# A fused attention and MLP kernel: the MLP's inner rows turned by VectorE and sixteen small DMAs instead of by TensorE

## The chip, the cores and the metric

The kernel runs on one core of a Trainium2 chip. The metric is the device time of one execution in microseconds (us). The engines are named as the profile names them: PE is TensorE (PEld its weight loads), DVE is VectorE, ACT is ScalarE, POOL is GpSimd, and SP is the engine that issues nearly all of the DMAs. Each engine takes its instructions strictly in the order in which the program lists them.

## What is computed

Attention over 8 batches, 8 heads, 576 positions and 64 columns a head, with a mask in blocks of 64, and then an MLP over the 4608 tokens whose 512 columns are the eight heads side by side. Inputs of the MLP are `w_in` (512 x 1024), `w_out` (1024 x 512) and a gain `g_ln` of 1024.

```python
scores = scale * np.matmul(q, k.transpose(0, 1, 3, 2))
scores = np.where(pos[:, None] // 64 >= pos[None, :] // 64, scores, -1e9)
attn = softmax(scores)                       # exp(s - max) / (sum + 1e-9)
x = np.matmul(attn, v)                       # -> (4608 tokens, 512)
h = x @ w_in
solu = h * softmax(h)
ln = (solu - mean) / np.sqrt(var + 1e-6) * g_ln
out = ln @ w_out
```

Products of numbers in fp32 are made from two parts, a high one rounded to `fp32r` and a low one with the rest: high x high, high x low and low x high, so each product is three matmuls.

## The kernel before

**Units of work.** Attention is done for 32 pairs of heads (4 pairs to a batch), the MLP for 36 tiles of 128 tokens; 4.5 tiles are the tokens of a batch. Every piece of work is entered with `op(engine, estimated time, function, reads, writes, key)` into a `Schedule` (lines 67 to 195). It plays the program through with its estimates and, whenever an engine is free, gives it the ready piece with the lowest key; the keys are a table of numbers (`PARAMS`). Some pieces have alternatives on another engine (`alts`), and the planner gives the piece to whichever is free first. The order that comes out is the order of the program on each engine. PSUM is eight banks: two double ones ("D", for `h` and for the last block of scores) and four single ones ("S", for all the rest). A piece that opens a bank has to wait until all readers of the bank's last content are done.

**Attention** (`attention(p)`, lines 396 to 559). `q` and `k` are loaded by four DMAs each in runs of 32 floats (line 404) so that a transposition of 32x32 blocks by DVE (line 428) yields the whole transposed matrix. The high part is made by ACT (429) or POOL (430), the low part by DVE (432, 434). PE makes the scores (452 for the last block, 458 for the rest, in which the two heads use one half of the array's rows each); DVE sets the mask and takes the maximum (477, 481), ACT makes the exponentials (485), DVE the reciprocals of the sums (493, 494), POOL or DVE multiplies (501). PE transposes these in 25 blocks (512), ACT copies the result to SBUF (389), PE multiplies by `v` (545), and ACT copies that (389 again) into `xt[b % 3]`, the transposed input of the MLP, of which three batches are kept.

**The MLP** (`moe(t)`, lines 562 to 656). High and low part of the tile of `xt` go into `xh` and `xl` (577, 581; two buffers each). 24 matmuls make `h` in a double bank (602). DVE takes the maximum (608), ACT the exponential into `ub[t % 2]` (609), DVE multiplies by `h` and sums (610), POOL or DVE subtracts the mean (612, 613), and ACT squares and sums into a scrap tile `junk` (614). Then the row of 1024 has to be transposed for the second product: for each half of four 128x128 blocks PE transposes into a bank (637), ACT copies the high part into `ch` (641), and DVE makes the low part `cl` (642). `ch` and `cl` have one buffer. 24 matmuls make the output (650), ACT scales it into `ob[t % 2]` (654), and a DMA stores it (656).

**The weights** come as 64-bit floats. For each of 16 pieces a DMA (339) and about eight operations on ACT, DVE and POOL (341 to 359) make the parts `wih`, `wil`, `woh`, `wol`. This happens beside the attention of the first pairs, and its scratch lies in `xt[2]` and `ob`.

Of the kernel before, what the change touches and what calls it, by code (L numbers as in the profile page):

```python
# [31 lines left out]
NPT = 2  # L32
SWITCH = 165.0
# [10 lines left out]
    "a_xh": 88.845, "a_xl": 84.956, "a_c": -284.662, "a_o": -306.432, "np": 32, "l0": 61.467,  # L44
    "a_cl": -142.34, "a_ai": 313.132, "aff": -118.477, "a_t3": 111.852, "a_cm": -246.845, "a_cg": -26.262,
    "a_qh": -9.099, "a_kl": 129.132,
# [151 lines left out]
def kernel(  # L198
# [17 lines left out]
    P = 128  # L216
# [25 lines left out]
    qz, kz, qt, kt = (sb(x, [S]) for x in ("qz", "kz", "qt", "kt"))  # L242
    vr = [sb(f"vr{i}", [5, P]) for i in range(2)]


    qh, ql, kh, kl = ([sb(f"{x}{i}", [S], F32R) for i in range(2)] for x in ("qh", "ql", "kh", "kl"))
    qdh, qdl = ([sb(f"{x}{i}", [P], F32R) for i in range(2)] for x in ("qdh", "qdl"))
# [83 lines left out]
    xtf = xt[2].rearrange("p a b -> p (a b)")  # L331
    wtmp = [(xtf[:, 0:512], xtf[:, 512:1024], ob[0]), (xtf[:, 1024:1536], xtf[:, 1536:2048], ob[1])]
# [59 lines left out]
    def attention(p):  # L392
# [5 lines left out]
        half = [slice(0, 64), slice(64, 128)]  # L398
        for nm, src, dst in (("kz", k, kz), ("qz", q, qz)):

            def load(nm=nm, src=src, dst=dst):
                for g in range(4):
                    dma = ACT if p == 0 and nm == "kz" else SP
                    dma.dma_start(
                        dst[32 * g : 32 * g + 32, :].rearrange("p (g d) -> p g d", d=32),
                        src[b0, 2 * hp + g // 2, :, 32 * (g % 2) : 32 * (g % 2) + 32].rearrange("(g p) d -> p g d", p=32),
                    )

            op("SP", 1600, load, w=[nm], key=(K["l0"] if p == 0 else p) + K["ld" + sfx], tail=2400)
# [16 lines left out]
        qh_, ql_, kh_, kl_, qdh_, qdl_ = qh[i], ql[i], kh[i], kl[i], qdh[i], qdl[i]  # L426
        for x, z, t, hi, lo, scale in (("k", kz, kt, kh_, kl_, 1.0), ("q", qz, qt, qh_, ql_, 0.125)):
            op("DVE", t_dve(S), lambda z=z, t=t: DVE.transpose(t, z), r=[x + "z"], w=[x + "t"], key=kk)
            op("ACT", t_act(S), lambda t=t, hi=hi, scale=scale: ACT.activation(hi, t, AF.Copy, scale=scale), r=[x + "t"], w=[(x + "h", i)], key=ke,
               alts=[("POOL", 0.836 * S + 243, lambda t=t, hi=hi, scale=scale: POOL.tensor_scalar(out=hi, in0=t, scalar1=scale, scalar2=1.0, op0=ALU.mult, op1=ALU.mult), K["a_qh"])])  # L430
            if x == "q":
                op("DVE", t_dve(S), lambda: DVE.scalar_tensor_tensor(out=ql_, in0=qt, scalar=0.125, in1=qh_.bitcast(F32), op0=ALU.mult, op1=ALU.subtract), r=["qt", ("qh", i)], w=[("ql", i)], key=ke, port=True)  # L432
            else:
                op("DVE", t_dve(S), lambda: DVE.tensor_tensor(out=kl_, in0=kt, in1=kh_.bitcast(F32), op=ALU.subtract), r=["kt", ("kh", i)], w=[("kl", i)], key=ke, port=True,
# [6 lines left out]
        for x, dst, src in (("qh", qdh_, qh_), ("ql", qdl_, ql_)):  # L441
            op("POOL", 300, lambda dst=dst, src=src: last(dst, src), r=[(x, i)], w=[(x + "d", i)], key=ke)

        for g, (kind, us, masks) in enumerate(groups):
# [15 lines left out]
            if us == [LAST]:  # L460
                d, md = 3 * (t_mm(320) + t_mm(256)), 0
                rd = [(x, i) for x in ("kh", "kl", "qhd", "qld")]
                tiles = [(sps[0], [(LAST, 192)])]
            else:
                d, md = sum(3 * t_row(128 * (i_ + 1)) for i_, _ in us), 2
                rd = [(x, i) for x in ("kh", "kl", "qh", "ql")]
# [65 lines left out]
        x2 = wkeys if b0 == 2 else []  # L532
# [22 lines left out]
        for ph in range(2):  # L555
            av = avs[ph]
            for rows, parts in xparts[ph]:
                for c_, q_, l_ in parts:
                    copy(2, l_, lambda rows=rows, av=av, c_=c_, q_=q_, l_=l_: (xt[b0 % 3][rows, hp, q_ : q_ + l_], PS(av)[rows, c_ : c_ + l_]), 1.0, [("xt", b0 % 3, hp, rows.start, q_)], ke, av, x2)


    def moe(t, key):
# [3 lines left out]
        while a < (t + 1) * P:  # L566
            bb = a // S
            e = min((t + 1) * P, (bb + 1) * S)
            segs.append((bb % 3, a - bb * S, e - bb * S, a - t * P, e - t * P))
# [44 lines left out]
        op("ACT", t_act(1024, 135), lambda: ACT.activation(junk, u, AF.Square, accum_out=m[:, 4:5]), r=[uk], w=[("m4", i)], key=key + K["sq"])  # L614
# [15 lines left out]
        op("POOL", 702, rstd, r=[("m7", i), ("m5", i)], w=[("m4", i), ("m3", i)], key=key + K["sq"])  # L630
        for hf in range(2):
            cps = newps("S")

            def ctrans(hf=hf, cps=cps):
                t_ = PS(cps)
# [65 lines left out]
```

## Time and profile before

| | |
|---|---|
| median of 3 runs | 790.3 us (789.97 to 790.9) |
| the profiled execution | 790.35 us, of which the span of the profile is 788.6 us |
| mean granted PE clock | 0.975 of full |
| busy share of PE, PEld | 96%, 76% |
| busy share of DVE, ACT, POOL | 60%, 66%, 43% |
| DMA | 198551 packets, 47.05 MB |

The profile is of one execution. Its windows divide the span into stretches and give for each engine the busy time in it. Its groups give the mean duration of one instruction of a line. Its chain follows back from the last instruction to whatever released it; where PE never waits, the chain simply is PE's work, so that the spacing of equal points in it is the period of the work.

### The profile page before, as it was taken

To read this page: it belongs to the slowest core of one execution; us is meant where nothing else is said; L and a number is where in the kernel's file an instruction comes from. 1 tells how busy PE (TensorE), PEld (TensorE's weight loads), DVE (VectorE), ACT (ScalarE), POOL (GpSimd) and SP (SyncE) were. 2 spreads that over 40 slices of the span, in tenths; PEclk is the share of its full clock that TensorE was granted. 3 is DMA by queue.
4 is the path that set the end of the run, shared out by engine and by line. 5 is a ranking of instruction groups with operands and counts; after the bars stand their busy time and mean duration, and the time that the engine had idled before them with its cause. 6 is when DMAs were issued, how large, how long until landed. Compare 5 with 4: busy or idle time off the path is not lost.

```text
span 788.6 us, 13834 instructions
## 1 busy us (share of the span) xinstructions
PE 760.3 (96%) x4687; PEld 595.4 (76%) x4687; DVE 471.7 (60%) x1191; ACT 521.6 (66%) x1349; POOL 341.7 (43%) x593
## 2 busy tenths in 40 slices
PE   4878999999999999999999999999999999999998
PEld 3656776887777777777777777787777878888886
DVE  5889998955666555555555666655554534444442
ACT  5788989876677676666777667677666654443332
POOL 4766857645444444444444444444445131121100
PEclk8787999999999999999999999999999999999999
DMA  9764653322222222222222222222200100000001
GB/s 185 144 137 118 120 120 88 61 59 59 58 43 48 59 49 55 59 46 59 59 59 59 59 46 48 55 51 54 59 23 22 30 14 27 26 16 28 14 27 41
DMA packets 198551, 47.05 MB, mean 60 GB/s; under 512 B 191824, under 2 KB 191824, under 8 KB 198480
## 3 DMA queue, kind: packets, MB, share of 16 engines
q1 hardware_dynamic: 196112, 45.87, 26.9%
q8 instruction: 37, 0.61, 0.3%
q10 hardware_dynamic: 2368, 0.30, 0.3%
q14 instruction: 34, 0.28, 0.1%
HBM read 36.70 MB, written 9.44 MB: 59 GB/s over the span
## 4 chain that ended last, share of the span: by engine, by line
PE 86%; ACT 5%; DVE 4%; DMA 2%; issue 1%; POOL 1%; SPq 0%; DVEq 0%; ACTq 0%; POOLq 0%
PE ps L650 25%; PE ps L602 25%; PE ps L512 10%; PE ps L545 9%; PE ps L458 8%; PE ps L637 4%; PE ps L452 3%; ACT pb L485 2%; DVE nm L481 1%; DMA ub<-in_moe_w_out_dram 1%; DMA kz<-in_k_dram 1%; DMA ub<-in_moe_w_in_dram 1%; POOL pb L501 0%; ACT xt L389 0%; DVE ql L432 0%
## 5 line engine op out<-in xcount | busy, mean ns | idle before, releaser
L501 POOL TENSOR_SCALAR pb<-pb,rz 128x384 f32<-128x384 f32 (+4 forms) x288 | 176.6, 629 | 241.4 <-DVE rz L494 227.2
L485 ACT ACTIVATE pb<-ps,nm 128x256 f32<-128x256 f32 (+4 forms) x288 | 155.1, 548 | 47.3 <-DVE nm L481 46.6
L389 ACT ACTIVATE pt<-ps 128x512 f32<-128x512 f32 (+1 forms) x224 | 108.5, 562 | 42.0 <-PE ps L512 41.6
L642 DVE TENSOR_TENSOR cl<-ps,ch 128x512 fp32r<-128x512 f32 x72 | 49.4, 686 | 142.7 <-ACT ch L641 142.7
L481 DVE TENSOR_REDUCE nm<-ps 128x1 f32<-128x256 f32 (+4 forms) x288 | 131.4, 509 | 2.1 <-PE ps L452 2.1
L512 PE MATMUL ps<-ident,pb 128*128 128x128 f32 x800 | 111.2, 287 | 11.2 <-POOL pb L501 6.3
L512 PEld LDWEIGHTS ps<-ident,pb 128*128 128x128 f32 x800 | 93.9, 146 | 24.6 <-POOL pb L501 9.7
L545 PE MATMUL ps<-pt,vr 128*64 128x320 f32 (+4 forms) x896 | 93.8, 360 | 0.3 <-ACT pt L389 0.3
L545 PEld LDWEIGHTS ps<-pt,vr 128*64 128x64 f32 x896 | 59.3, 137 | 34.4 <-issue 1.3
L602 PE MATMUL ps<-wih,xh 128*128 128x512 f32 x288 | 84.7, 416 | 0.2 <-ACT pb L485 0.2
L650 PE MATMUL ps<-woh,ch 128*128 128x512 f32 x288 | 83.4, 411 | 0.0
L602 PE MATMUL ps<-wil,xh 128*128 128x512 f32 x288 | 79.8, 399 | 0.0
L650 PE MATMUL ps<-wol,ch 128*128 128x512 f32 x288 | 79.0, 396 | 0.0
L602 PE MATMUL ps<-wih,xl 128*128 128x512 f32 x288 | 78.8, 395 | 0.0
L650 PE MATMUL ps<-woh,cl 128*128 128x512 f32 x288 | 78.6, 394 | 0.0
L625 POOL TENSOR_TENSOR ms<-ms,mhalf 128x1 f32<-128x1 f32 x36 | 19.8, 549 | 131.8 <-DVE ms L622 131.7
L641 ACT ACTIVATE ch<-ps 128x512 fp32r<-128x512 f32 x72 | 44.0, 611 | 49.5 <-PE ps L637 49.5
L458 PE MATMUL ps<-kh,qh 64*128 64x256 f32 (+3 forms) x256 | 57.4, 395 | 10.5 <-POOL qh L430 5.4
L602 PEld LDWEIGHTS ps<-wil,xh 128*128 128x128 f32 x288 | 54.9, 190 | 13.0
L654 ACT ACTIVATE ob<-ps,ms 128x512 f32<-128x512 f32 x36 | 24.8, 688 | 60.0 <-PE ps L650 54.3
L602 PEld LDWEIGHTS ps<-wih,xl 128*128 128x128 f32 x288 | 54.4, 189 | 12.9
L650 PEld LDWEIGHTS ps<-wol,ch 128*128 128x128 f32 x288 | 54.3, 188 | 12.8
(83 smaller groups left out, 1275.5 us busy)
## 6 DMA issues: line engine op xcount, KB each, us to landing
qz<-in_q_dram SPq DMA_DIRECT2D x128, 72.0 KB, 2.5
out_dram<-ob SPq DMA_DIRECT2D x36, 256.0 KB, 2.0
kz<-in_k_dram SPq DMA_DIRECT2D x124, 72.0 KB, 2.5
vr<-in_v_dram SPq DMA_DIRECT2D x64, 128.0 KB, 2.6
ub<-in_moe_w_in_dram SPq DMA_DIRECT2D x8, 512.0 KB, 4.2
ub<-in_moe_w_out_dram SPq DMA_DIRECT2D x8, 512.0 KB, 3.7
vr<-in_v_dram SPq DMA_DIRECT2D x32, 32.0 KB, 2.4
kz<-in_k_dram ACTq DMA_DIRECT2D x4, 72.0 KB, 3.8
```

Of the source, the lines that this page charges most:

```text
L389: op("ACT", t_act(n_), lambda: ACT.activation(aps()[0], aps()[1], AF.Copy, scale=scale), r=r, w=w, key=key, ps=ps, alts=[("DVE", t_dve(n_) ...
L458: PE.matmul(PS(sps[h])[:, off : off + 128 * (i_ + 1)], w_[half[h], 128 * i_ : 128 * i_ + 128], x_[half[h], 0 : 128 * (i_ + 1)], start=n_ = ...
L481: op("DVE", t_dve(wid[u]), lambda sp=sp, off=off, u=u: DVE.tensor_reduce(out=nm_[u], in_=PS(sp)[:, off : off + wid[u]], axis=AX.X, op=ALU. ...
L485: op("ACT", t_act(wid[u], 186), lambda sp=sp, off=off, u=u, zg=zg, zc=zc: ACT.activation(pb[:, poff[u] : poff[u] + wid[u]], PS(sp)[:, off ...
L501: op("POOL", 0.836 * nn + 243, lambda b=b, nn=nn, zg=zg, zc=zc: POOL.tensor_scalar(out=pb[:, poff[b] : poff[b] + nn], in0=pb[:, poff[b] : ...
L512: PE.transpose(t[:, (s_ - c0) * P : (s_ - c0 + 1) * P], pb[:, poff[b] + j * P : poff[b] + (j + 1) * P], ident)
L545: PE.matmul(PS(avs[ph])[half[h], 64 * o_ : 64 * (o_ + n_)], vt[:, j, 64 * h : 64 * h + 64], pt_.rearrange("p s q -> p (s q)")[:, 128 * s_ ...
L602: PE.matmul(o_, a_[:, c, :], w_[:, c, s_], start=(si == 0 and c == 0), stop=(si == 2 and c == NKI - 1))
L637: PE.transpose(t_[:, c * P : (c + 1) * P], u[:, (4 * hf + c) * P : (4 * hf + c + 1) * P], ident)
L641: op("ACT", t_act(512), lambda cs=cs, cps=cps: ACT.activation(ch[:, cs, :].rearrange("p c q -> p (c q)"), PS(cps), AF.Copy), w=[("ch", hf) ...
L642: op("DVE", t_dve(512), lambda cs=cs, cps=cps: DVE.tensor_tensor(out=cl[:, cs, :].rearrange("p c q -> p (c q)"), in0=PS(cps), in1=ch[:, cs ...
L650: PE.matmul(o_, a_[:, c, :], w_[:, c, :], start=(hf == 0 and si == 0 and c == 0), stop=(hf == 1 and si == 2 and c == 7))
```

## The change

1. **Transposition in the MLP, tiles 6 to 33** (28 of 36). DVE transposes the row of 1024 in 32x32 blocks from `ub` into a new tile `zb` (one buffer). SP then issues 16 DMAs, each of 32 partitions x 256 floats (pieces of 1 KB), that carry the blocks to their partitions in a new tile `ct` (one buffer). ACT and DVE make `ch` and `cl` from `ct` in SBUF; POOL and DVE are alternatives for `ch`, POOL for `cl`. Tiles 0 to 5 and 34 and 35 keep PE's transpositions.
2. **Attention's results in two batches** instead of three: `xt[b % 2]`. So the results of batch b can be written only where the tiles of batch b-2 have been read.
3. **Scratch.** `junk` is dropped and the squares go into `ob[t % 2]`; the weights' scratch lies in `zb`, `ct` and `ob`.
4. **The first four pairs** load `q` and `k` in runs of 64 floats (two DMAs of 128x4x64, and one of 64x2x64 into `kq`) and PE transposes them (9 blocks a pair) instead of DVE; their high and low parts are then read from PSUM.
5. **The table of keys** is another one. With it the multiplications by the reciprocals (501) go mostly to DVE (none of 288 before, 205 now), the subtraction of the mean too (27 of 36 instead of 14), and 24 of the `kl` go to POOL.

The core of the diff:

```diff
+NQK = 2
+XB = 2
+PEQ = 4
+PET, PEL = 6, 34
 PARAMS = {
-    "nd": 2, "ld": -112.86, "lv": 9.571, "q": 88.586, "qe": 132.144, "s": 58.329, "se": -84.684,
+    "nd": 2, "ld": -336.409, "lv": -194.807, "q": 8.649, "qe": 317.465, "s": 21.981, "se": -51.803,
...
-    xt = [sb(f"xt{i}", [NP, S]) for i in range(3)]
+    xt = [sb(f"xt{i}", [NP, S]) for i in range(XB)]
...
+    zb = sb("zb", [DFF])
+    ct = sb("ct", [4, NKO, 32])
     ch = sb("ch", [NKO, P], F32R)
     cl = sb("cl", [NKO, P], F32R)
     ob = [sb(f"ob{i}", [DM]) for i in range(2)]
-    junk = sb("junk", [DFF], mybir.dt.bfloat16)
...
+                if peq:
+                    for h in range(2):
+                        dma.dma_start(
+                            dst[:, 0:512].rearrange("p (c d) -> p c d", c=4)[:, :, 64 * h : 64 * h + 64],
+                            src[b0, 2 * hp + h, 0:512, :].rearrange("(c p) d -> p c d", p=P),
+                        )
...
+            op("PE", 109 * 5, lambda: trans(kz, pk, True), r=["kz", "kzq", "qzq"], key=kk, opens=pk)
+            op("PE", 109 * 4, lambda: trans(qz, pq, False), r=["qz"], key=kk, opens=pq)
...
-        op("ACT", t_act(1024, 135), lambda: ACT.activation(junk, u, AF.Square, accum_out=m[:, 4:5]), r=[uk], w=[("m4", i)], key=key + K["sq"])
+        op("ACT", t_act(1024, 135), lambda: ACT.activation(ob[i].bitcast(mybir.dt.bfloat16), u, AF.Square, accum_out=m[:, 4:5]), r=[uk], w=[("m4", i), ("ob", i)], key=key + K["sq"])
...
+        if PET <= t < PEL:
+            op("DVE", t_dve(DFF), lambda: DVE.transpose(zb.rearrange("p (r c i) -> p r c i", r=4, i=32), u.rearrange("p (c r i) -> p r c i", r=4, i=32)), r=[uk] + (wkeys if t == PET else []), w=["zb"], key=key + K["ct"])
+
+            def place():
+                for r_ in range(4):
+                    for a_ in range(4):
+                        SP.dma_start(ct[32 * r_ : 32 * r_ + 32, a_, :, :], zb[32 * a_ : 32 * a_ + 32, 256 * r_ : 256 * r_ + 256])
+
+            op("SP", 2800, place, r=["zb"], w=["ct"], key=key + K["ct"], tail=2400)
         for hf in range(2):
+            cs = slice(hf * 4, hf * 4 + 4)
+            h_, l_ = (x[:, cs, :].rearrange("p c (a j) -> p a c j", a=4) for x in (ch, cl))
+            if PET <= t < PEL:
+                c_ = ct[:, :, cs, :]
+                op("ACT", t_act(512), lambda c_=c_, h_=h_: ACT.activation(h_, c_, AF.Copy), r=["ct"], w=[("ch", hf)], key=key + K["ce"],
...
+                op("DVE", t_dve(512), lambda c_=c_, h_=h_, l_=l_: DVE.tensor_tensor(out=l_, in0=c_, in1=h_.bitcast(F32), op=ALU.subtract), r=["ct", ("ch", hf)], w=[("cl", hf)], key=key + K["ce"], port=True,
...
+                continue
```

How it moves the instructions is shown at three places. The first is PE near the end of the program, when attention is over: the last matmuls of one tile's `h` (`xl_132`) and what stands between them and the next tile's `h` (`xh_129`). Before:

```order
L602 MATMUL ps_61<-wih,xl_132 128x512 x4
L650 MATMUL ps_65<-woh,ch 128x512 x4
L650 MATMUL ps_65<-wol,ch 128x512 x4
L650 MATMUL ps_65<-woh,cl 128x512 x4
L637 MATMUL ps_64<-ident,ub_133 128x128 x4
L650 MATMUL ps_65<-woh,ch 128x512 x4
L650 MATMUL ps_65<-wol,ch 128x512 x4
L650 MATMUL ps_65<-woh,cl 128x512 x4
L637 MATMUL ps_66<-ident,ub_133 128x128 x4
L602 MATMUL ps_62<-wih,xh_129 128x512 x4
```

And now:

```order
L640 MATMUL ps_61<-wih,xl_132 128x512 x4
L705 MATMUL ps_64<-woh,ch 128x512 x4
L705 MATMUL ps_64<-wol,ch 128x512 x4
L705 MATMUL ps_64<-woh,cl 128x512 x4
L705 MATMUL ps_64<-woh,ch 128x512 x4
L705 MATMUL ps_64<-wol,ch 128x512 x4
L705 MATMUL ps_64<-woh,cl 128x512 x4
L640 MATMUL ps_62<-wih,xh_129 128x512 x4
```

The two groups of four transpositions of `ub` are gone, so that PE's row is `h` of one tile and the output of an earlier one in turn. From the end of a tile's `h` to the start of its output there stand, as before, two outputs and two `h` of other tiles.

The second place is DVE in the same stretch. Before, from the multiplication of one tile (`ub_134`) to the maximum of the next (`ms_140`):

```order
L610 SCALAR_TENSOR_TENSOR ub_134,ms_141<-ps_61,ub_134 128x1024
L642 TENSOR_TENSOR cl<-ps_64,ch 128x512
L611 TENSOR_SCALAR ms_141<-ms_141 128x1
L613 TENSOR_SCALAR ub_134<-ub_134,ms_141 128x1024
L642 TENSOR_TENSOR cl<-ps_65,ch 128x512
L622 TENSOR_SCALAR ms_141<-ms_141 128x1
L608 TENSOR_REDUCE ms_140<-ps_62 128x1
```

And now:

```order
L648 SCALAR_TENSOR_TENSOR ub_134,ms_142<-ps_61,ub_134 128x1024
L686 TENSOR_TENSOR cl<-ct,ch 128x4x4x32
L649 TENSOR_SCALAR ms_142<-ms_142 128x1
L651 TENSOR_SCALAR ub_134<-ub_134,ms_142 128x1024
L686 TENSOR_TENSOR cl<-ct,ch 128x4x4x32
L670 STREAM_TRANSPOSE zb<-ub_134 128x1024
L660 TENSOR_SCALAR ms_142<-ms_142 128x1
L646 TENSOR_REDUCE ms_141<-ps_62 128x1
```

The two `cl` are of the tile before, whose blocks the DMAs have carried to `ct`; the transposition of this tile's row into `zb` comes behind them, since `zb` and `ct` have one buffer each.

The third place is SP's row in the middle of the program, where attention and MLP run beside each other. Before, one pair and one tile:

```order
L656 DMA out_dram<-ob_138 128x512
L404 DMA kz<-in_k_dram 32x18x32 x4
L404 DMA qz<-in_q_dram 32x18x32 x4
L413 DMA vr_83<-in_v_dram 128x4x64 x2
L417 DMA vr_83<-in_v_dram 64x2x64
L656 DMA out_dram<-ob_137 128x512
```

And now:

```order
L675 DMA ct<-zb 32x256 x16
L711 DMA out_dram<-ob_140 128x512
L434 DMA vr_83<-in_v_dram 128x4x64 x2
L438 DMA vr_83<-in_v_dram 64x2x64
L675 DMA ct<-zb 32x256 x16
L425 DMA kz<-in_k_dram 32x18x32 x4
L425 DMA qz<-in_q_dram 32x18x32 x4
L711 DMA out_dram<-ob_139 128x512
```

The sixteen DMAs stand ahead of the loads of a later pair, which cannot be issued before them.

More of the change, by code (lines that the diff above doesn't have):

```diff
@@ L428, in attention @@
+        for x, z, t, hi, lo, scale in () if peq else (("k", kz, kt, kh_, kl_, 1.0), ("q", qz, qt, qh_, ql_, 0.125)):
             op("DVE", t_dve(S), lambda z=z, t=t: DVE.transpose(t, z), r=[x + "z"], w=[x + "t"], key=kk)
-            op("ACT", t_act(S), lambda t=t, hi=hi, scale=scale: ACT.activation(hi, t, AF.Copy, scale=scale), r=[x + "t"], w=[(x + "h", i)], key=ke,
+            op("ACT", t_act(S), lambda t=t, hi=hi, scale=scale: ACT.activation(hi, t, AF.Copy, scale=scale), r=[x + "t"], w=[(x + "h", iq)], key=ke,
@@ L461, in attention @@
                 d, md = 3 * (t_mm(320) + t_mm(256)), 0
[L462 removed]
+                rd = [(x, iq) for x in ("kh", "kl", "qhd", "qld")]
                 tiles = [(sps[0], [(LAST, 192)])]
@@ L558, in attention @@
                 for c_, q_, l_ in parts:
-                    copy(2, l_, lambda rows=rows, av=av, c_=c_, q_=q_, l_=l_: (xt[b0 % 3][rows, hp, q_ : q_ + l_], PS(av)[rows, c_ : c_ + l_]), 1.0, [("xt", b0 % 3, hp, rows.start, q_)], ke, av, x2)
+                    copy(2, l_, lambda rows=rows, av=av, c_=c_, q_=q_, l_=l_: (xt[b0 % XB][rows, hp, q_ : q_ + l_], PS(av)[rows, c_ : c_ + l_]), 1.0, [("xt", b0 % XB, hp, rows.start, q_)], ke, av)
     def moe(t, key):
```

63 lines of the change are left out of this document (42 added, 21 removed), and 12 rows, old and new, of the table PARAMS.

## Prediction

> **What bounds the kernel now.** I read the page first (busy shares, then the chain of work that ended last), then the windows, to see where PE is not busy.
>
> ```profile
> PE 760.3 (96%) x4687; PEld 595.4 (76%) x4687; DVE 471.7 (60%) x1191; ACT 521.6 (66%) x1349; POOL 341.7 (43%) x593
> ...
> PE 86%; ACT 5%; DVE 4%; DMA 2%; issue 1%; POOL 1%; SPq 0%; DVEq 0%; ACTq 0%; POOLq 0%
> ```
>
> ```profile
> 0.00:160.00 160.00, 135.55 (x889) 102.93 (x890) 135.37 (x331) 130.22 (x357) 104.06 (x178) 0.88 0.59 122
> 160.00:620.00 460.00, 460.00 (x2982) 360.38 (x2981) 267.19 (x705) 321.44 (x859) 210.40 (x369) 1.00 0.25 51
> 620.00:784.00 164.00, 164.00 (x818) 131.83 (x817) 69.11 (x155) 69.28 (x135) 27.23 (x46) 1.00 0.06 23
> 664.10:676.16 12.06, 12.06 (x57) 9.84 (x57) 5.22 (x11) 4.76 (x9) 2.04 (x3) 1.00 0.06 22
> 341.14:362.58 21.44, 21.44 (x140) 16.80 (x140) 12.53 (x33) 14.99 (x42) 9.78 (x17) 1.00 0.27 54
> ```
>
> The columns of a window are its length and the busy time of PE, PEld, DVE, ACT and POOL, then granted clock, DMA share and GB/s. There are three stages. Up to 160 us PE is idle for 160.0 - 135.55 = 24.45 us at a mean clock of 0.88: the weights are being prepared and DVE (135.4) and ACT (130.2) are nearly full. From 160 to 784 PE is busy in all of it at full clock, first with a pair and a tile in 21.44 us (fifth row), then with tiles alone in 12.06 us (fourth row). In these 624 us only PE's own work counts: an instruction taken off PE is gain, unless something else then comes late.
>
> **What PE loses.** In the last stage the chain, in order of time, shows 24 matmuls of `h` as one piece, and the next one 12.06 us later.
>
> ```profile
> by line: PE ps L650 25.0%; PE ps L602 24.8%; PE ps L512 10.3%; PE ps L545 9.4%; PE ps L458 8.5%; PE ps L637 4.4%; PE ps L452 3.3%; ACT pb L485 2.3%; issue 1.4%; DVE nm L481 1.1%; DMA ub<-in_moe_w_out_dram 1.0%; DMA kz<-in_k_dram 0.7%; DMA u
> ...
> 664.10 5.58 PE ps L602 x24
> 676.16 5.59 PE ps L602 x24
> ```
>
> The output also has 24 matmuls of 512 columns, so it is worth 5.59 us too, and 12.06 - 2 x 5.59 = 0.88 us is left for the eight transpositions. The chain's shares give a second value: L637 with 4.4% of 788.6 is 34.7 us, 0.96 for each of 36 tiles. I take the lower one: 28 x 0.88 = 24.6 us less, all in the stages where PE is full. By the order, blocks of scores (the matmuls that use half the array's rows) begin 81 times now and 92 times before.
>
> ```profile
> PEld ps L458 <- issue: 24.0, 69, 0.4
> ```
>
> Weight loads stood idle for 24.0 / 69 = 0.35 us ahead of such a block. 11 fewer are 3.8 us if that is on PE's path and nothing if the matmul before hides it; I take 1.0.
>
> **What the others get.** A transposition of 576 takes 0.77 us and a maximum of 1024 takes 1.22.
>
> ```profile
> L428 DVE STREAM_TRANSPOSE qt<-qz 128x576 f32<-128x576 f32 x32 | 24.5, 766 | 1.1 <-DMA qz<-in_q_dram 0.8
> L608 DVE TENSOR_REDUCE ms<-ps 128x1 f32<-128x1024 f32 x36 | 43.8, 1216 | 31.1 <-PE ps L602 31.0
> L501 POOL TENSOR_SCALAR pb<-pb,rz 128x512 f32<-128x512 f32 x64 | 55.8, 884 | 9.2 <-DVE rz L494 4.2 <-ACT pt L389 1.7 <-PE ps L512 0.5
> L343 DVE TENSOR_SCALAR xt<-ub 128x512 f32<-128x512 f32 x9 | 3.8, 419 | 0.3 <-DMA ub<-in_moe_w_out_dram 0.3
> L642 DVE TENSOR_TENSOR cl<-ps,ch 128x512 fp32r<-128x512 f32 x72 | 49.4, 686 | 142.7 <-ACT ch L641 142.7
> L641 ACT ACTIVATE ch<-ps 128x512 fp32r<-128x512 f32 x72 | 44.0, 611 | 49.5 <-PE ps L637 49.5
> ```
>
> One of 1024 should take 1.24 us, 34.7 us in all. The 205 multiplications that come from POOL cost DVE at most about 0.42 us each (the 512 wide one; POOL needs 0.88), some 62 us over all widths. In the middle stage that is 1.24 + 2.0 us more a pair, less 0.6 for the `kl` that go: about 15.5 us of DVE in a period of 20.5 (12.53 of 21.44 before). It stays below PE's 20.5, so I cost it at nothing; that cover would be gone if DVE had to stand still for 5 us in every period. `ch` and `cl` read SBUF instead of PSUM; I leave them at 0.61 and 0.69.
>
> **The sixteen DMAs** are the unknown price. No DMA of before goes from SBUF to SBUF or has 32 rows. The nearest are these, with the time that SP spends on each issue (second column; the middle two rows hold four DMAs and one):
>
> ```profile
> 311.19 0.37 SPq L656 DMA_DIRECT2D out_dram<-ob  x1
> ...
> 319.57 1.93 SPq L404 DMA_DIRECT2D qz<-in_q_dram  x4
> ...
> 322.69 0.61 SPq L417 DMA_DIRECT2D vr<-in_v_dram  x1
> ```
>
> ```profile
> out_dram<-ob SPq DMA_DIRECT2D x36, 256.0 KB, 2.0
> ...
> vr<-in_v_dram SPq DMA_DIRECT2D x64, 128.0 KB, 2.6
> ```
>
> A plain store of 128 rows takes 0.37 us to issue and lands 2.0 us later; the worst, with three dimensions, takes 0.61, and 2.6 is a late landing. Sixteen in a row are then P = 16 x 0.37 + 2.0 = 7.9 us from `zb` to a whole `ct`, and 16 x 0.61 + 2.6 = 12.4 at worst. If an issue went with the number of rows it would be a quarter of 0.37, and P = 3.5. I take 7.9, since the store has the same plain form. The Trainium skill, on the page "DMA: Bandwidth & Descriptors", section "Issuing engines are not separate DMA queues", says that the sequencer's time to start a DMA is usually small beside the DMA itself. By that, P would be little over 2.0 and the two stall terms below would be zero; the rows above speak against it for sixteen issues in a row.
>
> Does P reach PE? In the last stage one tile's turn through `ct` is: P, `ch`, then the store's copy of the tile before, the second `ch`, `cl`, and the next transposition.
>
> ```profile
> 712.01 0.69 ACT L654 ACTIVATE ob<-ps,ms 128x512 f32<-128x512 f32 x1 [2.19 <-PE ps L650]
> ...
> 712.59 0.59 ACT L641 ACTIVATE ch<-ps 128x512 fp32r<-128x512 f32 x1
> 712.73 0.15 DVE L611 TENSOR_SCALAR ms<-ms 128x1 f32<-128x1 f32 x1 [1.91 <-ACT ob L654]
> 712.92 0.76 DVE L613 TENSOR_SCALAR ub<-ub,ms 128x1024 f32<-128x1024 f32 x1
> ```
>
> That is P + 0.61 + 0.69 + 0.59 + 0.69 + 1.24 and some 0.4 for handing over: P + 4.2 = 12.1 us, against 2 x 5.59 = 11.2 of PE. The turn is longer by 0.9 us, over the 8 tiles that are left then 7.4 us. The start has a reserve: between a tile's `h` and its output PE has four blocks, 4 x 5.59 = 22.4 us, and the way through maximum, exponential, product, mean, transposition, P, `ch`, `cl` sums up to about 17. So some 5.4 of the 7.4 are absorbed and 2.0 us remain.
>
> In the middle stage the turns come 15 to 20 us apart, so the turn itself does not bind; but DVE and ACT take their work in order, and while a `cl` waits for `ct`, the maxima of the scores queue behind it, and PE waits for those. By the order, in some nine of the 20 tiles there are only 4 to 8 us of DVE work between the transposition and its `cl`, where 7.9 + 0.6 are needed. The same wait is there before:
>
> ```profile
> DVE cl L642 <- ACT ch L641: 142.7, 27, 11.0
> ```
>
> DVE stood still 27 times at `cl`, up to 11.0 us, and PE was full all the while. So PE has work in hand for waits of this size; I take 2.0 us and keep 0 to 14.
>
> SP itself: the sixteen issues of 5.9 us stand ahead of loads of a pair (eight of 0.48 and three of `v`, about 6 us of issue). Together with 0.37 a store that is some 12 of 20 us. Loads may come 6 us later, but the buffers they fill are free a period ahead. The squares now also wait until the store of two tiles before has left `ob`, which it did a whole tile ago, and the weights' scratch in `zb` and `ct` is free before tile 6; both cost nothing.
>
> **The start.** PE makes 36 transpositions more in it; at 0.23 us (15 of them in 3.46) they are 8.3 us. DVE loses eight of 0.77, 6.2 us, and the first loads have half as many pieces.
>
> ```profile
> 1.70 3.46 PE L283 MATMUL ps<-ident 128*128 128x128 f32 x15 [1.70 <-POOL ident masks.py:199]
> ...
> PE ps L458 <- POOL qh L430: 5.4, 1, 5.4
> ```
>
> PE's first scores waited 5.4 us for `qh`, and PE has 24.45 idle us to hide in. Counting rows, DVE has the same work behind it at the same progress (ten pairs and four or five tiles) in both orders. I take 0, from -8 to +5.
>
> **Against the change** speaks the Trainium skill, page "VectorE: DVE Perf Modes", sections "The three transpose paths" and "Rules for kernel authors": VectorE's transposition stays within 32x32 blocks, and for a whole 128x128 one should use TensorE where PSUM will do as the target. Here the result was read from PSUM, so the page would keep it there; the trace has PE full for 624 us and DVE at 58%, and the page does not weigh that. By it alone nothing would be gained, about 790.
>
> **The sum**, against the profiled execution's 790.35 us (its span of 788.6 and 1.75 around it; the median of the runs is 790.3): 790.35 - 24.6 - 1.0 + 0 + 2.0 + 2.0 = 768.75, or 768.8.
>
> **Rivals.**
> - *The start gets shorter.* Shorter loads and multiplications of half the time shorten the chain of the first pairs by the 5 to 8 us above: 768.8 - 7 = 762. Against it stands that DVE and ACT are nearly full there anyway.
> - *Half the gain is given back in the middle stage,* to 781. With two batches, the last copies into `xt` of a batch's first two pairs have to wait for a tile two batches back, and hold two of four single banks of PSUM meanwhile; by the order that is about 30 us long at pair 24. With two banks left, a group of four transpositions of 0.44 us comes round every (0.44 + 0.6 + 0.4) / 2 = 0.72 us, 0.28 later each; 13 groups are 3.6 us a batch, about 12 where it happens in three or four of the six batches it can. For it speaks that DVE is at 76% and has less time to catch up.
> - *Slower: the issue costs what the worst row says.* P = 12.4 makes the turn 16.6 us, 5.4 over PE's 11.2: 8 x 5.4 - 5.4 = 38 us, and 1 us for each of 20 tiles before: 790.35 - 25.6 + 58 = 823. The gain is eaten from about 8 x (turn - 11.2) - 5.4 + 4 = 26 on, a turn of 14.6 and P = 10.4, which is 0.5 us an issue. Against it: plain forms took 0.37.
> - *The gain is eaten just so,* within 790 +- 1.6, by an issue of about 0.5 us; here the rule of the transpose paths would put it.
>
> **How the numbers follow.** Forecast 0.58 (763 to 776), shorter start 0.10, half given back 0.20 (774 to 787), slower 0.09, no change 0.03. Faster by more than 0.2% (1.6 us, about what a measurement of this kernel can tell) is 0.58 + 0.10 + 0.20 = 0.88. The range leaves out slower, no change, and the outer half of the shorter start: 757 to 786. The predicted time is the forecast's, 768.8.
>
> **What the profile after would show.** PE full from about 160 us to the end; the chain with L637's successor at 1% (8 tiles and the last copies) instead of 4.4%; two equal points of the last stage 11.2 to 11.5 us apart; about 20.5 us for a pair and a tile; sixteen issues in some 6 us on SP and a landing about 2 us later. I would be wrong if the last stage's period is over 12 us, if PE waits for maxima or for `pt` in the middle stage for more than 5 us in all, if the sixteen issues take over 8 us, or if PE's idle time before 160 us moves by more than 8 us.

## The result, and the profile after

| | before | after |
|---|---|---|
| median | 790.1 us (788.0 to 790.9, 4 runs) | 856.5 us (854.1 to 859.8, 4 runs) |
| profiled execution, span | 790.35, 788.6 us | 857.65, 855.8 us |
| mean granted PE clock | 0.975 | 0.938 |

The ratio is 1.085 with a 95% interval of 1.080 to 1.089: 66 us slower, where 21.5 less were forecast. The page of the kernel after, busy shares, the chain by engine and the issue of the new DMAs:

```profile
PE 776.1 (91%) x4499; PEld 598.1 (70%) x4499; DVE 565.1 (66%) x1404; ACT 525.9 (61%) x1355; POOL 236.7 (28%) x402
...
PE 36%; SPq 21%; DVE 18%; ACT 10%; DMA 9%; issue 5%; POOL 1%; ACTq 0%; DVEq 0%; POOLq 0%
...
ct<-zb SPq DMA_DIRECT2D x448, 32.0 KB, 1.8
```

PE was 86% of the chain before and is 36% now; SP's queue has gone from 0% to 21%. PE is busy for 16 us more (776.1 against 760.3) although it makes 188 matmuls fewer. The windows of the kernel after, cut at the last matmul with `v` (712.3 us; 650.8 before):

```profile
0.00:160.00 160.00, 144.24 (x962) 110.86 (x963) 142.01 (x359) 134.18 (x367) 83.75 (x152) 0.90 0.54 122
160.00:712.00 552.00, 511.20 (x3060) 392.42 (x3060) 368.62 (x938) 349.12 (x912) 138.49 (x224) 0.95 0.28 64
712.00:855.80 143.80, 120.67 (x482) 94.81 (x478) 54.46 (x107) 42.56 (x79) 14.50 (x27) 0.92 0.16 49
```

Before, PE was busy in all of the middle stage at clock 1.00. Now it stands still for 40.8 us there and for 23.1 in the last stage, and in both its clock is below 1.00. The turn of one tile through `ct` in the last stage, from the timeline:

```profile
741.48 10.24 SPq L675 DMA_DIRECT2D ct<-zb  x16
...
756.22 1.24 DVE L670 STREAM_TRANSPOSE zb<-ub 128x1024 f32<-128x1024 f32 x1
...
757.52 10.01 SPq L675 DMA_DIRECT2D ct<-zb  x16
...
769.16 0.63 ACT L683 ACTIVATE ch<-ct 128x512 fp32r<-128x512 f32 x1 [8.56 <-DMA ct<-zb]
...
769.82 0.69 DVE L686 TENSOR_TENSOR cl<-ct,ch 128x512 fp32r<-128x512 f32 x1 [7.38 <-ACT ch L683]
...
769.84 1.19 PE L705 MATMUL ps<-woh,ch 128*128 128x512 f32 x4 [2.68 <-ACT ch L683]
...
773.18 10.01 SPq L675 DMA_DIRECT2D ct<-zb  x16
```

Sixteen issues take 10.0 us, 0.63 each, not 0.37. From the end of the transposition (757.46) to `ch` it is 11.7 us, and the next sixteen start 15.7 us after these; the sets of this stage follow each other by 15.4 to 16.2 us. PE needs 11.2 for the two products and waits for `ch`. The middle stage, also from the timeline:

```profile
450.29 0.63 ACT L683 ACTIVATE ch<-ct 128x512 fp32r<-128x512 f32 x1 [6.77 <-DMA ct<-zb]
450.83 1.24 ACT L397 ACTIVATE xt<-ps 128x256 f32<-128x256 f32 x5
...
450.95 0.69 DVE L686 TENSOR_TENSOR cl<-ct,ch 128x512 fp32r<-128x512 f32 x1 [5.11 <-ACT ch L683]
...
451.24 1.78 PE L551 MATMUL ps<-ident,pb 128*128 128x128 f32 x6 [3.38 <-ACT xt L397]
451.56 1.28 DVE L520 TENSOR_REDUCE nm<-ps 128x1 f32<-128x512 f32 x2
```

ACT stands still for 6.77 us at `ch` and DVE for 5.11 at `cl`; five copies into `xt` and the maxima stood queued behind them, and PE had waited 3.38 us for a bank that those copies free. The waits from 160 to 712 us (total, times, longest):

```profile
ACT ch L683 <- DMA ct<-zb: 68.1, 11, 8.4
DVE cl L686 <- ACT ch L683: 56.8, 12, 11.6
...
PE ps L497 <- ACT pb L524: 16.2, 9, 5.9
```

### The profile page after: what moved, and what is told of

Same layout as the page of the kernel before. It is cut to its first block, busy times and chain, and to the rows that moved or that the text cites. A ratio compares the mean times of both kernels' runs of the same rounds, so it can differ in the third digit from the quotient of the medians.

```text
span 855.8 us, 14074 instructions
## 1 busy us (share of the span) xinstructions
PE 776.1 (91%) x4499; PEld 598.1 (70%) x4499; DVE 565.1 (66%) x1404; ACT 525.9 (61%) x1355; POOL 236.7 (28%) x402
## 4 chain that ended last, share of the span: by engine, by line
PE 36%; SPq 21%; DVE 18%; ACT 10%; DMA 9%; issue 5%; POOL 1%; ACTq 0%; DVEq 0%; POOLq 0%
SPq L675 20%; PE ps L705 11%; PE ps L640 8%; PE ps L551 5%; DMA ct<-zb 5%; PE ps L583 4%; PE ps L497 4%; DVE nm L520 4%; ACT pb L524 3%; DVE pb L541 3%; DMA out_dram<-ob 2%; PE ps L491 1%; DVE cl L686 1%; ACT ob L652 1%; ACT ob L709 1%
## 5 line engine op out<-in xcount | busy, mean ns | idle before, releaser
L524 ACT ACTIVATE pb<-ps,nm 128x384 f32<-128x384 f32 (+4 forms) x288 | 155.7, 553 | 44.0 <-DVE nm L520 43.2
L520 DVE TENSOR_REDUCE nm<-ps 128x1 f32<-128x384 f32 (+4 forms) x288 | 132.7, 508 | 9.6 <-PE ps L491 9.6
L686 DVE TENSOR_TENSOR cl<-ct,ch 128x512 fp32r<-128x512 f32 x56 | 40.0, 714 | 139.4 <-ACT ch L683 115.1
L683 ACT ACTIVATE ch<-ct 128x512 fp32r<-128x512 f32 x56 | 35.5, 634 | 145.6 <-DMA ct<-zb 134.4
L705 PE MATMUL ps<-woh,ch 128*128 128x512 f32 x288 | 88.8, 432 | 21.1 <-ACT ch L683 19.3
L640 PE MATMUL ps<-wih,xh 128*128 128x512 f32 x288 | 89.3, 434 | 0.0
L497 PE MATMUL ps<-kh,qh 64*128 64x384 f32 (+3 forms) x256 | 63.1, 400 | 24.8 <-ACT pb L524 17.5
L705 PEld LDWEIGHTS ps<-woh,ch 128*128 128x128 f32 x288 | 53.0, 200 | 37.5 <-ACT ch L683 22.3
L541 DVE TENSOR_SCALAR pb<-pb,rz 128x128 f32<-128x128 f32 (+4 forms) x205 | 76.7, 437 | 0.9
L474 POOL TENSOR_TENSOR kl<-kt,kh 128x576 fp32r<-128x576 f32 x24 | 36.0, 1502 | 133.1 <-ACT kh L468 133.1
L705 PEld LDWEIGHTS ps<-wol,ch 128*128 128x128 f32 x288 | 57.4, 199 | 13.9
```

The costliest lines, as they stand in the source:

```text
L474: alts=[("POOL", 1380, lambda: POOL.tensor_tensor(out=kl_, in0=kt, in1=kh_.bitcast(F32), op=ALU.subtract), K["a_kl"])])
L497: PE.matmul(PS(sps[h])[:, off : off + 128 * (i_ + 1)], w_[half[h], 128 * i_ : 128 * i_ + 128], x_[half[h], 0 : 128 * (i_ + 1)], start=n_ = ...
L520: op("DVE", t_dve(wid[u]), lambda sp=sp, off=off, u=u: DVE.tensor_reduce(out=nm_[u], in_=PS(sp)[:, off : off + wid[u]], axis=AX.X, op=ALU. ...
L524: op("ACT", t_act(wid[u], 186), lambda sp=sp, off=off, u=u, zg=zg, zc=zc: ACT.activation(pb[:, poff[u] : poff[u] + wid[u]], PS(sp)[:, off ...
L541: alts=[("DVE", nn / 1.92 + 128, lambda b=b, nn=nn, zg=zg, zc=zc: DVE.tensor_scalar(out=pb[:, poff[b] : poff[b] + nn], in0=pb[:, poff[b] : ...
L640: PE.matmul(o_, a_[:, c, :], w_[:, c, s_], start=(si == 0 and c == 0), stop=(si == 2 and c == NKI - 1))
```

## The experiments

Each was timed beside the kernel before on the same chip. The theory after the result was: the length of the way from `zb` to `ct` costs the time, by the turn in the last stage and by ACT and DVE standing still in order in the middle. Its rivals were the rest of the change, and the order, which was planned for a way of 5.2 us (2.8 of issue and 2.4 of landing).

**The DMAs alone.** A kernel of nothing but DMAs, in batches of one shape.

> Only DMAs, nothing of the kernel's computation (the output is zeros): batches of one shape each on SP's queue, then sixteen of 32x256 from SBUF to SBUF on ACT's and on POOL's queue. Theory (the price lies in the issue of a DMA of this form): sixteen of 32x256 from SBUF to SBUF take SP 0.55 to 0.7 us each here too, with nothing else running, 9 to 11 us a batch, while a store of 128x512 stays at 0.33 to 0.40. Rival (the price comes from the kernel around it: SP or the rings are held up by other traffic): alone they take 0.30 to 0.40 us each, 5 to 6.5 us a batch. Which of rows, length of a row, or SBUF as source and target sets it is open: if rows, 64x256 and 128x256 cost more than 32x256; if the ends, 32x256 from and to DRAM cost about 0.37.

The duration of one issue by lines (min/median/max in ns): 32x256, 64x256, 128x256, 32x1024 and 32x64 from SBUF to SBUF, then 32x256 from DRAM to SBUF, 32x256 from SBUF to DRAM and 128x512 from SBUF to DRAM on SP; and 32x256 from SBUF to SBUF on POOL:

```profile
L51 SPq DMA_DIRECT2D d<-src x16: 588/596/658, 2.1 to 11.8; - x16
...
L54 SPq DMA_DIRECT2D d<-src x8: 591/594/596, 12.4 to 16.9; - x8
...
L56 SPq DMA_DIRECT2D d<-src x4: 595/599/600, 17.5 to 19.5; - x4
...
L58 SPq DMA_DIRECT2D dfull<-src x4: 588/588/597, 20.1 to 22.0; - x4
...
L61 SPq DMA_DIRECT2D dn<-src x16: 588/589/595, 22.6 to 32.2; - x16
...
L64 SPq DMA_DIRECT2D dload<-in_q_dram x16: 397/419/577, 0.7 to 38.5; - x16
...
L70 SPq DMA_DIRECT2D out_dram<-src x16: 314/420/962, 39.4 to 53.4; - x16
...
L74 SPq DMA_DIRECT2D out_dram<-src x32: 445/645/1010, 55.9 to 78.5; - x32
...
L82 POOL DMA_DIRECT2D dpool<-src x16: 496/497/628, 53.3 to 60.8; - x16
```

The price belongs to the DMA, not to the kernel around it. Sixteen of line 51 took 10.28 us with almost nothing else running. Between SBUF and SBUF it goes neither with rows (32 to 128) nor with their length (64 to 1024 floats); it goes with where the data lies: 0.59 us from SBUF to SBUF, 0.42 from DRAM or to it for the same 32x256. POOL issues the same DMA in 0.50. One part of the theory failed: stores of 128x512, expected at 0.33 to 0.40, took 0.65 in a row of 32, while the DMA engines were full (share 1.01 from 56 to 79 us). So the 0.37 of a single store was not its price in a long row either.

**TensorE for tiles 6 to 33 too.**

```diff
-PET, PEL = 6, 34
+PET, PEL = 36, 36
```

> Tiles 6 to 33 too are transposed by TensorE; all else of the change (two batches, first pairs, scratch, table of keys) stays. Theory (the length of the sixteen DMAs costs the time): PE is nearly full again from 160 us on, a tail period of 12.1 us, and 785 to 805 us in all, since the table was not made for this. Rival (two batches and the new order lose the time): 825 to 860 us, with PE's waits in the middle stage staying.

789.55 us, ratio 0.9996 (0.998 to 1.001). Two batches, the loads of the first pairs, the scratch and the new keys come to nothing together. The whole loss hangs on the new transposition.

**The planner told the measured price.**

```diff
-            op("SP", 2800, place, r=["zb"], w=["ct"], key=key + K["ct"], tail=2400)
+            op("SP", 10000, place, r=["zb"], w=["ct"], key=key + K["ct"], tail=1800)
```

> Only the planner's estimate of the sixteen DMAs is changed, from 2.8 us of issue and 2.4 of landing to 10.0 and 1.8; the work is the same. Theory (length): the tail cannot be mended by an order, its period stays at 15.4 to 15.8 us, and only the middle gains; 825 to 850 us. Rival (the order, planned with a wrong price, costs the time): under 805 us, and the tail's period falls below 13.

810.3 us, ratio 1.026 (1.024 to 1.028): under the theory's band, above the rival's. Both have a part. Its windows:

```profile
160.00:641.00 481.00, 473.57 (x3007) 366.74 (x3003) 357.95 (x927) 342.26 (x902) 131.66 (x213) 1.00 0.31 70
641.00:809.00 168.00, 137.46 (x550) 107.54 (x544) 65.69 (x128) 51.34 (x92) 17.93 (x32) 0.91 0.17 52
```

With the right price the middle stage has only 7.4 us of idle PE and clock 1.00 again, and ACT's waits at `ch` for the DMAs come to 8.4 us (longest 2.6) instead of 68.1. Sixteen DMAs are still made for each of the 18 tiles that fall into this stage (21 in the kernel after), so it is the waiting and not the transfers themselves that costs PE the middle. More tiles are left for the end (ten sets of DMAs begin after attention, seven in the kernel after), and there a turn comes every 14.4 us (two sets start at 699.66 and 714.08). So an order can hide the way beside attention, and this one does not hide it in the last stage: 30.5 us of PE idle.

**Fewer of the sixteen, in the unchanged order.** The loop stops after ten or six DMAs, so that six or ten of a tile's sixteen blocks are not carried over; the order on PE, DVE, ACT and POOL is that of the kernel after.

```diff
-                for r_ in range(4):
-                    for a_ in range(4):
+                for n_ in range(10):
+                    r_, a_ = divmod(n_, 4)
...
```

> Ten of the sixteen DMAs, all else and the order on PE, DVE, ACT and POOL as in the changed kernel; six of the sixteen blocks of a tile are not brought over, so the values are wrong. At the 0.63 us an issue of the DMAs alone, the way from zb to ct is 10 x 0.63 + 1.8 = 8.1 us, nearly the forecast's 7.9. Theory (the price of the issue is the only step that failed): the other terms of the prediction hold, the tail's period is 11.5 to 12.3 and the time 764 to 785 us. Rival (the terms for the middle stage fail too, even at that price): over 795 us, with PE idle over 15 us between 160 us and the end of attention.

> As the run with ten, with six DMAs (ten blocks of a tile are not brought over, the values are wrong): 6 x 0.63 + 1.8 = 5.6 us, close to the 5.2 that the planner was told. Theory: PE is the bound of the tail, period 11.2 to 11.6, no waits in the middle, 760 to 772 us. Rival: over 785 us.

| DMAs | way, worked out | attention ends | turn or period in the last stage | median | ratio to before |
|---|---|---|---|---|---|
| 6 | 5.6 us | 654.6 | 11.16 | 768.2 | 0.973 (0.970 to 0.976) |
| 10 | 8.1 us | 670.6 | 11.6 to 12.6 | 782.2 | 0.992 (0.989 to 0.995) |
| 16 | 11.8 us | 712.3 | 15.4 to 16.2 | 856.5 | 1.085 (1.080 to 1.089) |

Windows of six, then of ten:

```profile
160.00:655.00 495.00, 488.09 (x3082) 379.85 (x3077) 369.92 (x941) 352.89 (x922) 138.21 (x227) 1.00 0.27 58
655.00:766.70 111.70, 107.82 (x472) 87.14 (x471) 55.09 (x105) 43.65 (x76) 14.60 (x25) 1.00 0.12 40
```

```profile
160.00:671.00 511.00, 493.43 (x3072) 382.76 (x3071) 369.75 (x941) 351.63 (x918) 138.67 (x225) 0.99 0.28 61
671.00:783.00 112.00, 108.17 (x472) 87.12 (x471) 54.41 (x105) 42.18 (x76) 14.44 (x25) 1.00 0.15 49
```

These three kernels differ in the number of DMAs alone. From six to sixteen the middle stage gets 57 us longer (552 for 495) and the last 32 (143.8 for 111.7). Of the 57, 33.9 are idle PE (40.8 against 6.9) and 23.1 are nearly the same matmuls (3060 and 3082 in the windows) taking longer, at a granted clock of 0.95 instead of 1.00 (511.2 busy against 488.1). At ten, close to the forecast's way, the last stage is as long as at six although a turn is 0.4 to 1.4 us longer, so the reserve that the prediction counted on was there; the middle loses 16 us. The time lies in the theory's band there, but near its upper end, and the rival's idle time of over 15 us is there too (17.6 against 6.9): the price was not the only step that failed.

**A way through DRAM with five DMAs.**

```diff
+    zd = ctx.enter_context(tc.tile_pool(name="zp", bufs=1, space=bass.MemoryType.DRAM)).tile([P, DFF], F32, name="zd")
...
-                        SP.dma_start(ct[32 * r_ : 32 * r_ + 32, a_, :, :], zb[32 * a_ : 32 * a_ + 32, 256 * r_ : 256 * r_ + 256])
+                SP.dma_start(zd, zb)
+                for a_ in range(4):
+                    SP.dma_start(ct[:, a_, :, :].rearrange("p c j -> p (c j)"), zd[32 * a_ : 32 * a_ + 32, :].rearrange("p (r x) -> r p x", r=4))
```

> The sixteen DMAs become five: one store of the whole tile to DRAM and four loads of 128 rows x 1 KB. Estimate from the rows of the kernel after: 0.35 of issue + 2.0 + 4 x 0.4 to 0.6 + 2.5 = 6.4 to 7.3 us instead of 11.8. Theory (length): the turn through ct falls to 10.5 to 11.5 us, so that the tail's period falls from 15.6 to 11.2 to 12.3, and the middle's waits at ch and cl shrink too: 775 to 810 us. Rival (two batches, order): the tail gains 8 x 4 = 32 us at most and nothing of the middle, 825 us or more.

826.2 us, ratio 1.047 (1.044 to 1.049): outside the theory's band, because the way got hardly shorter. Timeline of one tile in the last stage:

```profile
761.16 0.33 SPq L674 DMA_DIRECT2D zd<-zb  x1
...
763.80 2.19 SPq L676 DMA_DIRECT2D ct<-zd  x4
...
771.68 0.63 ACT L684 ACTIVATE ch<-ct 128x512 fp32r<-128x512 f32 x1 [7.39 <-DMA ct<-zd]
```

The issues are cheap (2.5 us), but the loads go out 2.3 us after the store's issue and land 5.7 us after their own (765.99 to 771.68): 10.6 us from `zb` to `ch`, where 6.4 to 7.3 were estimated. In the last stage the way is 10.3 to 11.7 us (11.4 to 12.2 in the kernel after) and a turn comes every 14.3 to 15.6. In the middle, where ACT's wait at `ch` ended with the DMAs, the median way is 11.1 us against 12.9. The run is still 30 us faster than the kernel after, 22 of them before attention ends (690.6). From ten DMAs to sixteen, 3.7 us of way cost the middle 42 us; by that rate 1.8 us are worth some 20 (an estimate). So the shorter way can account for nearly all of the 22 us; whether SP's shorter time adds to it is not shown.

**Who stands still in the middle.** The copy to `ch`, the subtraction for `cl`, or both are issued to POOL at the same place of the program; the order elsewhere is unchanged.

```diff
-                op("ACT", t_act(512), lambda c_=c_, h_=h_: ACT.activation(h_, c_, AF.Copy), r=["ct"], ...
+                op("ACT", t_act(512), lambda c_=c_, h_=h_: POOL.tensor_scalar(out=h_, in0=c_, scalar1=1.0, scalar2=1.0, op0=ALU.mult, op1=ALU.mult), r=["ct"], ...
-                op("DVE", t_dve(512), lambda c_=c_, h_=h_, l_=l_: DVE.tensor_tensor(out=l_, ...
+                op("DVE", t_dve(512), lambda c_=c_, h_=h_, l_=l_: POOL.tensor_tensor(out=l_, ...
```

> The copy from ct to ch is issued to POOL instead of ACT at the same place of the program; the order on PE, DVE and SP is that of the changed kernel, all sixteen DMAs stay. So ACT no longer stands still at ch, with exponentials and copies of pt behind it; DVE still stands still at cl. Theory A (ACT's standing starves PE in the middle stage): attention ends before 680 us instead of 712, the tail stays at 15.4 to 16, 815 to 830 us. Theory B, the prediction's own picture (DVE's standing at cl, with maxima behind it, does it): attention ends at 700 us or later, 845 us or more.

> The subtraction that makes cl is issued to POOL instead of DVE at the same place; ACT still makes ch and stands still there. POOL needs about 1.3 us for it instead of 0.69, so the tail's turn is some 1.2 us longer, 16.5 to 17 us. Theory A: attention ends at 700 us or later, 850 us or more. Theory B: attention ends before 680 us, 825 to 840 us.

> Both edits at once: neither ACT nor DVE waits for the DMAs, only POOL, whose own work (subtractions for k and for x) then queues behind. Theory A and B alike, if the standing of an engine in order is the way in which the length of the DMAs reaches PE: attention ends at 650 to 670 us with the length of the DMAs unchanged, the tail's turn is 16.5 to 17, 810 to 830 us. Rival (the transfers or the loads behind them on SP's queue cost PE the time): attention ends at 700 us or later.

| on POOL | attention ends | median | ratio to before |
|---|---|---|---|
| `ch` | 707.6 | 856.9 | 1.086 (1.083 to 1.089) |
| `cl` | 710.3 | 855.2 | 1.083 (1.080 to 1.085) |
| both | 689.7 | 833.9 | 1.056 (1.051 to 1.061) |

Theories A (ACT alone) and B (DVE alone) both fell: freeing one engine gives nothing, freeing both gives 22.6 us in the middle, so one standing engine is enough to starve PE. But that run too missed its band (650 to 670) and is 35 us short of what six DMAs show. There POOL stands still at `ch` in their place (88.7 us, with its own work behind it), so the run cannot tell whether these 35 us come from standing too or from something else. With `ch` on POOL, the waits up to 708 us were:

```profile
ACT pb L524 <- DVE nm L520: 96.8, 41, 10.6
...
DVE cl L686 <- DMA vr<-in_v_dram: 32.4, 4, 11.2
...
DVE cl L686 <- POOL ch L683: 31.4, 6, 10.3
PE ps L497 <- ACT pb L524: 26.0, 10, 6.0
```

DVE still stands at `cl`. The rows that name `vr` are the same wait: in the longest, `cl` starts at 287.15 us, as POOL's first `ch` (286.50, 0.60 long) ends. ACT, freed from `ch`, now waits for DVE instead: its exponentials (`pb`) wait 96.8 us for maxima (`nm`; 38.3 in the kernel after), and PE waits for the banks that they hold.

**SP's queue.** Two tries at what is left: own scratch for the squares, in the kernel after and with both on POOL, and all sixteen issued by POOL.

```diff
-ACT.activation(ob[i].bitcast(mybir.dt.bfloat16), u, AF.Square, accum_out=m[:, 4:5])
+ACT.activation(junk, u, AF.Square, accum_out=m[:, 4:5])
```

```diff
-                        SP.dma_start(ct[32 * r_ : 32 * r_ + 32, a_, :, :], zb[32 * a_ : 32 * a_ + 32, 256 * r_ : 256 * r_ + 256])
+                        POOL.dma_start(ct[32 * r_ : 32 * r_ + 32, a_, :, :], zb[32 * a_ : 32 * a_ + 32, 256 * r_ : 256 * r_ + 256])
```

> The squares go into a scratch tile of their own again instead of ob, so that they do not wait for the store of two tiles before; the order is unchanged. Prediction's step (this costs nothing): 852 to 860 us. Rival (ACT's 23.5 us of waiting at the squares is on PE's path, in the tail above all): 835 to 848 us.

> As the run with ch and cl on POOL, and the squares go into a scratch tile of their own. There the store of a tile stands behind the sixteen issues on SP, and ACT waits for that store at the squares (22.9 us in the middle), with the exponentials behind it. Theory (a third way for the length to reach PE, through SP's order): attention ends at 665 to 682 us instead of 690, 815 to 828 us. Rival (those waits are covered): attention ends at 687 us or later, 830 us or more.

> All sixteen DMAs are issued by POOL instead of SP at the same place of the program; ch stays on ACT and cl on DVE. The DMAs alone gave 16 x 0.50 + 3.2 = 11.2 us from zb to ct there, nearly the 11.8 of SP, so the standing at ch and cl stays, but SP's loads and stores are not behind the sixteen issues any more. Theory (standing of ACT and DVE in order carries most of it): attention ends at 695 us or later, tail's turn 14.5 to 15.5, 835 to 855 us. Rival (the loads and stores behind on SP carry most of it): attention ends before 680 us.

Own scratch gave 852.2 us (1.080, 1.077 to 1.082), and with both on POOL 830.8 (1.053, 1.050 to 1.057), attention's end 685.4. The differences (some 4 and 3 us) are not clear of noise, since the intervals overlap, and 852.2 is inside the band for "costs nothing". So the squares' wait for the store costs at most some 4 us, and the theory of a third way was wrong. With all sixteen on POOL it was 847.9 us (1.074, 1.072 to 1.076). The last stage gained, with a turn of 13.7 to 13.9 us (once 16.5) where 14.5 to 15.5 were expected. Attention ended at 716.3, no earlier, although ACT's waits at `ch` fell from 68.1 to 39.6 us; so loads and stores behind the issues do not carry most of it. POOL itself held up PE there (11.8 us of waits for its multiplications), so this does not clear SP's queue entirely. How the 31 us divide that the middle still has over six DMAs (685.4 against 654.6, with both on POOL and own scratch) is not settled.

**Versions that beat both kernels.** TensorE from tile 24 on, with the right price; and eight DMAs on SP with eight on POOL, planned for 5.0 + 1.8 and 4.0 + 3.2 us.

```diff
-PET, PEL = 6, 34
+PET, PEL = 6, 24
```

```diff
+            op("SP", 5000, place, r=["zb"], w=[("ct", 0)], key=key + K["ct"], tail=1800)
+            op("POOL", 4000, lambda place=place: place(POOL, 8, 16), r=["zb"], w=[("ct", 1)], key=key + K["ct"], tail=3200)
...
```

With two queues the planner also lets DVE work while POOL issues. All three versions have orders of their own.

> The planner is told the measured price (10.0 us of issue, 1.8 of landing), and TensorE transposes from tile 24 on, which are the tiles that come after attention; 18 tiles keep the DMAs. Theory (the turn through ct bounds the tail alone once the order knows the price): 18 x 0.88 = 15.8 us off PE, 5 to 8 us lost in the middle as in the run with the right price, a tail's period of 12.1: 778 to 786 us, below both kernels. Rival (DVE and the DMAs cost PE more in the middle than they free): 790 us or more.

> Eight of the sixteen DMAs are issued by SP and eight by POOL at the same time, the planner told 5.0 + 1.8 and 4.0 + 3.2 us. From the DMAs alone: SP 8 x 0.64 + 1.9 = 7.0, POOL 8 x 0.50 + 3.2 = 7.2 us from zb to ct instead of 11.8. Theory (length of the turn): the tail's period is 11.2 to 11.8, attention ends about where it does with the right price or earlier, 768 to 785 us. Rival (POOL's DMAs are held up by its own work or by DVE, so that the turn stays over 14 us): 800 us or more.

> The version with eight issues by SP and eight by POOL, and the squares' own scratch tile, newly planned. If the squares' wait for the store still costs PE something there: 757 to 762 us. If not: 762 to 767 us.

780.05 us with TensorE at the end (0.989, 0.987 to 0.991), in its band, and **763.65 us with two queues** (0.968, 0.966 to 0.970), which is the fastest and 4 us below its band; own scratch on top gave 766.4 (0.972, 0.970 to 0.974), no gain. Two queues, last stage and windows:

```profile
660.09 4.95 SPq L675 DMA_DIRECT2D ct<-zb  x8
...
660.57 4.00 POOL L675 DMA_DIRECT2D ct<-zb  x8 [8.20 <-ACT ob L652]
...
666.75 0.63 ACT L684 ACTIVATE ch<-ct 128x512 fp32r<-128x512 f32 x1 [2.17 <-DMA ct<-zb]
```

```profile
160.00:648.00 488.00, 483.16 (x3058) 375.92 (x3057) 369.64 (x926) 349.42 (x913) 219.07 (x401) 1.00 0.32 73
648.00:762.00 114.00, 110.67 (x484) 89.50 (x484) 60.57 (x115) 45.15 (x79) 37.45 (x79) 1.00 0.20 60
```

The way is 6.7 us (660.03 to 666.75; 6.4 to 7.9 over the stage), the period mostly 11.16, and PE stands still for 4.8 us in the middle. The forecast's gain is there once the way is short and the planner knows it.

## Why the prediction was wrong, point by point

- **The failed step is the price of the sixteen DMAs:** "I take 7.9, since the store has the same plain form". It was 16 x 0.63 + 1.8 = 11.8. The store was the wrong neighbour: its data goes to DRAM, and the price depends on that and not on the form or the rows. The worst row, 0.61, fitted by luck. Nor is it so that no DMA of before has 32 rows: the loads of `q` in the prediction's own fence have them (`32x18x32`, four in 1.93 us). At 0.48 each they spoke against a price by rows, and would have given 9.7. The sentence of the Trainium skill that it cited, on the page "DMA: Bandwidth & Descriptors", section "Issuing engines are not separate DMA queues", erred further to the same side: here the sequencer's 10.0 us for sixteen are over five times the 1.8 of a landing. What that section grants to several issuing engines, the sequencer's time, was the gain here.
- **The second failed step is the middle stage:** "So PE has work in hand for waits of this size; I take 2.0 us". At nearly the forecast's own way (ten DMAs) it was 16 us beside six, and at 11.8 it was 57. The inference was drawn from DVE's row alone. Its longest wait, 11.0 us, was not in the middle stage at all but came after it; and beside it stood another row of the kernel before. Rows of 160 to 651 us, then one of 651 to 789:

```profile
DVE cl L642 <- ACT ch L641: 127.9, 24, 6.5
ACT ch L641 <- PE ps L637: 39.2, 21, 2.0
```

```profile
DVE cl L642 <- ACT ch L641: 14.8, 3, 11.0
```

  The 11.0 us ended at 652.74 us, when the last matmul with `v` (650.8) had begun and no maximum of scores was left to queue behind it; in the middle the longest was 6.5. And before, ACT never stood at `ch` for more than 2.0 us, and then for PE's own transpositions, so that exponentials and copies kept coming while DVE waited. Now both stand, ACT for up to 8.4 us and DVE for up to 11.6. Two at once are not needed: with `ch` on POOL DVE alone stood at `cl`, up to 11.2 us, and attention ended nearly as late (707.6). Nor was the order asked what way it had been planned for: told 11.8 instead of 5.2, it gave 46 us back.
- **The turn in the last stage was right as a formula.** P + 4.2 gives 16.0 at 11.8 and 12.3 at 8.1; 15.4 to 16.2 and 11.6 to 12.6 were measured.
- **What comes off PE was right:** 11.16 for 12.06 us a tile is 0.90 (forecast 0.88), at most 25.2 us for 28. From TensorE throughout (789.55) to six DMAs (768.2) it was 21.3. The 1.0 us for fewer blocks of scores could not be told apart.
- **Start, scratch, DVE.** With TensorE throughout, everything else came to zero, as taken. PE's idle time before 160 us fell from 24.45 to 15.8, more than the 8 allowed, but PE's own 8.3 us of transpositions went into it and nothing ended earlier. The squares' wait cost at most some 4 us, which the intervals do not tell from nothing. A transposition of 1024 took 1.24 as estimated. The multiplications kept DVE busy for 76.7 us instead of 62; two queues reached 763.65 us with them.
- **The rivals.** The slow one had the mechanism and nearly the size of a turn (16.6), but priced the middle at 20 us and the clock at nothing, so 823 instead of 856. Its point of decision, P = 10.4, has the right sign on both sides of the runs: 8.1 gained a little, 11.8 lost. Half given back for want of a third batch does not show: the rest of the change cost nothing by itself.
- **The Trainium skill's rule of the transpose paths** ("VectorE: DVE Perf Modes", "Rules for kernel authors") held for the change as made, which lost 66 us, and not for it with two queues, where PE is the bound and 26 us are gained.

The sum as the runs have it, by profiled spans: six DMAs 766.7, + 57 in the middle (34 idle, 23 clock), + 32 in the last stage (19 idle, 13 clock) = 855.7, of 855.8 measured.

## What to carry to other kernels

Price many small DMAs in a row by what their queue takes to issue them, measured for the same source and target, and lay that against the period of the engine that is to be relieved. A wait that was harmless on one in-order engine says nothing of a longer one, of one at another stage or of one on another engine: look at what ends it, which engines it newly stops and what is queued behind. And where a planner sets the order, see that it knows the price of the new step; then ask whether a second queue halves it.

## What the runs showed of the hardware

- On SP, an issue takes 0.59 us from SBUF to SBUF for 32 to 128 rows and for 64 to 1024 floats, and 0.42 from DRAM or to it for 32x256; 32 stores of 128x512 in a row took 0.65 each. POOL's queue takes 0.50. SP's and POOL's queues issue side by side (4.95 and 4.00 us for eight each at the same time).
- Four loads of 128x256 from a tile just stored in DRAM, each with its rows from four column groups, were there only 5.5 to 6.3 us after their last issue (eight tiles of the last stage), not the 2.5 estimated.
- Where PE had gaps its clock was lower: where it stood still for 40.8 of 552 us the granted clock was 0.95, and nearly the same work took 23.1 us longer than where it stood for 6.9 of 495 at 1.00. The sum of the gaps alone does not set it: with `cl` on POOL 40.4 of 550 us came with 0.97. The page "TensorE: Matmul & The Clock Gate" of the Trainium skill, Part 1, says that the clock is let through by recent activity and halved after an idle window; these rows agree, but no run here varies the gaps alone.
